# Value products of two pairs of heads as one block in an attention and top-1 expert kernel

## The chip, the core and the metric

The kernel runs on one core of a Trainium2 chip, as one launch. The metric is the device time of that core in microseconds, from first instruction to last. Engines are named as in the profile: PE (TensorE, matmuls; PEld are its weight loads), DVE (VectorE), ACT (ScalarE), POOL (GpSimd), SP (SyncE, which issues most DMA transfers here).

## The reference

```python
scores = scale * np.matmul(q, k.transpose(0, 1, 3, 2))      # 8 batches, 8 heads, 576 x 64
cum = np.cumsum(np.maximum(s, 0.0), axis=-1)
bias = -(cum[:, :, :, None] - cum[:, :, None, :])
scores = np.where(causal, -1e9, scores + np.minimum(bias, 0.0))
scores = scores - np.max(scores, axis=-1, keepdims=True)
attn = np.exp(scores)
attn = attn / (np.sum(attn, axis=-1, keepdims=True) + 1e-09)
x = np.matmul(attn, v)              # -> 4608 tokens x 512
...
e_idx = np.argmax(x @ w_gate + modality_bias[modality_id], axis=1)   # 8 experts
# for each token: its one expert, 512 -> 1024 (relu) -> 512, times the softmax weight of that expert
```

## The kernel before

Two batches of the same head make a pair: 32 pairs of heads, numbered 0 to 31, eight (the heads) to a group of two batches. Group after group is scored, and when a group is done its tokens are given to experts and scattered to lists in DRAM (`lists<-x,di` on POOL, line 841). The expert stage follows the attention.

Each pair takes nine steps (`run`). A step scores one tile of 128 queries, in the order `ORDER = (3, 7, 2, 6, 8, 1, 5, 0, 4)`: tiles 0 to 3 belong to the one batch of the pair, 4 to 7 to the other, tile 8 holds the last 64 queries of both. A score is a product in two parts, high (L376: `KA`, `QH`) and low (L398: `KB`, `QL`); tile 8 has eight of 288 columns (L416, L417). It goes to one of four PSUM banks named `sp`, in turn. DVE takes the score from there, masks it and finds the row's minimum (L400); ACT makes the exponentials and their sums (L431). `LAG = 3` steps later PE transposes the tile (L451, into one of two banks `pt`, or L466), and ACT or DVE copies it to `PT` (L455), of which there are two, for even and odd pairs.

When all nine tiles of a pair are in `PT`, `whole` issues the pair's value products (L547), two matmuls of 64 columns of V on each half of the array: 512 columns of sums in the bank `o`, the last 64 of queries in an `sp` bank called `ox`. `TD = 1` puts them one step after the last transpose, in the fifth of the nine steps of the next pair. Then ACT copies the sums to `oT` (L554), DVE the last 64 columns (L557), and PE projects `oT` by `pw` and `pq` (L350, into `xo`), which also brings them back to token order; `XLAG = 6` steps lie between the two parts of the projection.

The operands of pair p+1 are prepared while pair p is scored (`prep`): POOL rounds `KA` and `QH` (L326, two halves each) and subtracts for `QL` and the lower `KA` (L330, two halves each). There are two of each tile, so POOL must wait until pair p−1 has been scored; the raw q and k are loaded one pair earlier still. SP issues the loads, the copy of the upper half of `KA` to `KB`, and the rows of the bias (`place`: `KB<-ek`, `QL<-ek`, for pairs under 8 from SBUF, `KB<-ekd`, `QL<-eqd` later). The order on every engine is that in which the program issues, but for places where `issue_after` fixes it.

The last pair, 31, has its products in two parts (`tail`).

Of the kernel before, what the change touches and what calls it, by code (L numbers as in the profile page):

```python
# [7 lines left out]
F32 = mybir.dt.float32  # L8
# [4 lines left out]
ALU = mybir.AluOpType  # L13
# [4 lines left out]
P = 128  # L18
KW = 576
XW = 72  # L20
# [4 lines left out]
ORDER = (3, 7, 2, 6, 8, 1, 5, 0, 4)  # L25
LAG = 3
XLAG = 6
TD = 1
SPB = 4
# [13 lines left out]
class Attn:  # L43
# [3 lines left out]
    def __init__(self, ctx, tc, qkv, s, ident, wg):  # L47
        nc = tc.nc
        self.nc, self.tc, self.qkv, self.ident = nc, tc, qkv, ident
        c = self.const = ctx.enter_context(tc.tile_pool(name="aconst", bufs=1))  # L50
# [10 lines left out]
        self.KB = [c.tile([P, 2, KW], F32R, name=f"KB{u}") for u in range(2)]  # L61
        self.PT = [c.tile([P, 2, PTW], F32, name=f"PT{u}") for u in range(2)]
        self.oT = c.tile([P, 640], F32, name="oT")
        self.pw = c.tile([P, 8, 2 * XW], F32, name="pw")
        self.pq = c.tile([P, 8, XW], F32, name="pq")
        self.mk = c.tile([P, 800], F32, name="mk")
# [2 lines left out]
        self.pe, self.wall, self.last = [], None, None  # L69
        self.raw, self.V = {}, {}  # L70
        self.hold, self.act, self.sp = [None], None, None
# [12 lines left out]
        nc.sync.dma_start(self.wg, wg.rearrange("p (h e) -> p h e", e=8))  # L84
        self.V[0] = self.load_v(0)

# [16 lines left out]
        nb, last = t1.tile([P, 5], F32, name="nb"), 0.0  # L103
        end = t1.tile([P, 2], F32, name="end")
        hold = ExitStack()
        for g, w in enumerate((256, 256, 64)):
            nc.vector.tensor_tensor_scan(cum[g][:, :w], s8[:, 256 * g:256 * g + w], zz.broadcast_to([P, w]), last, ALU.add, ALU.add)
            n = (w + P - 1) // P
            nc.vector.tensor_scalar(nb[:, 2 * g:2 * g + n], cum[g][:, 0:w:P], -1.0, None, ALU.mult)
            if g < 2:  # L110
                last = end[:, g:g + 1]
# [8 lines left out]
        for c in (3, 2, 1, 4, 0):  # L120
            n = min(P * (c + 1), KW)
# [25 lines left out]
        with self.tc.issue_after(self.sp):  # L147
            self.V[1] = self.load_v(1)
        self.more = {6: self.units}
# [144 lines left out]

    def consts(self):
        nc = self.nc
        nc.gpsimd.memset(self.oT[:, 512:], 0.0)
        for t in self.PT:
            nc.vector.memset(t[64:, :, PTW - 64:], 0.0)

# [8 lines left out]
        return raw  # L309

    def load_v(self, pi):
        V = self.ld.tile([P, 2, 5, 64], F32, name="V")
        self.nc.sync.dma_start(V, self.qkv[pi, :, 4 * KW:].rearrange("p (a j d) -> p a j d", a=2, j=5))
        return V

# [48 lines left out]
    def start(self, pi, x):  # L364
        st = dict(pi=pi, h=pi % 8, x=x, s={}, high={}, PT=self.PT[pi % 2], V=self.V.pop(pi, None))
        st["mx"] = self.sm.tile([P, 10], F32, name="mx")
        st["sums"] = self.sm.tile([P, 9], F32, name="sums")
        return st
# [156 lines left out]
        if g:  # L525
            nc.vector.tensor_scalar(x[2][:, 0, :, h], xo[:, 4 * XW:5 * XW].rearrange("p (d r) -> p d r", r=2), rs[:, 8:9], None, ALU.mult)

    def whole(self, st):

        nc = self.nc  # L530
        V, PT, x, h = st["V"], st["PT"], st["x"], st["h"]
        for _ in range(TD):
            yield
        o, ox = st["o"], self.ps1.tile([P, 512], F32, name="sp", bufs=SPB)
        oT = self.oT

        pe, self.pe = self.pe, []
        for j in range(5):
            for q0, q1, t, b in ((P * j, 512, o, 0), (512, KW, ox, 512)):
                if q0 == q1:  # L540
                    continue
                for ab in range(2):
                    r = slice(64 * ab, 64 * ab + 64)
                    with ExitStack() as after:
                        for i in pe:
                            after.enter_context(self.tc.issue_after(i))
                        m = nc.tensor.matmul(t[r, q0 - b:q1 - b], V[:, ab, j, :], PT[:, ab, PTS * j + q0 if j < 4 else PTW - 64:PTS * j + q1 if j < 4 else PTW], start=j == 0, stop=j == (4 if b else 3))  # L547
                pe = [m.ins]
        self.wall = m.ins
        rs = self.sm.tile([P, 9], F32, name="rs")  # L550
        with self.tc.issue_after(self.hold[0]), self.tc.issue_after(self.act):
            nc.scalar.activation(rs, st["sums"], AF.Identity, bias=self.eps[:, :1])
            nc.vector.reciprocal(rs, rs)
        nc.scalar.copy(oT[:, :512], o)  # L554
        for ab in range(2):
            r = slice(64 * ab, 64 * ab + 64)
            nc.vector.tensor_copy(oT[r, 512 + 64 * ab:576 + 64 * ab], ox[r, :64])  # L557
        yield
        xo = self.xo
        for g in (1, 0):  # L560
            for u in range(2):
                c = 2 * g + u
                with self.tc.issue_after(self.pe[-1]):
                    self.pw_(xo[:, 2 * XW * u:2 * XW * u + 2 * XW], oT[:, P * c:P * c + P], self.pw[:, h, :], start=True, stop=True)
            if g:
                self.pw_(xo[:, 4 * XW:5 * XW], oT[:, 512:], self.pq[:, h, :], start=True, stop=True)
            src = xo[:, :4 * XW].rearrange("p (t d) -> p t d", t=4)
            rv = rs[:, 4 * g:4 * g + 4].unsqueeze(2).broadcast_to([P, 4, XW])
            nc.vector.tensor_tensor(x[g][:, :, :, h], src.rearrange("p t (d r) -> p t d r", r=2), rv.rearrange("p t (d r) -> p t d r", r=2), ALU.mult)
            if g:  # L570
                nc.vector.tensor_scalar(x[2][:, 0, :, h], xo[:, 4 * XW:5 * XW].rearrange("p (d r) -> p d r", r=2), rs[:, 8:9], None, ALU.mult)
                for _ in range(XLAG if st["pi"] % 8 < 7 and st["pi"] < 30 else 1):
                    yield

    def strict(self, k):

# [2 lines left out]
    def run(self, npair, newx, done, setup):  # L579

        bg = self.bg = []
        seq = [(pi, i) for pi in range(npair) for i in ORDER]
        sts = {}
        prev, prepg, n = [], None, len(seq)
        for k in range(n + LAG + 9):
            if k < n:
                pi, i = seq[k]
                if k % 9 == 0:
                    sts[pi] = self.start(pi, newx(pi // 8) if pi % 8 == 0 else sts[pi - 1]["x"])
                    prepg = self.prep(pi + 1) if pi + 1 < npair else None  # L590
                with self.behind() if pi or not self.pe else self.tc.issue_after(self.pe[-1]), self.strict(k):
                    exps = self.score(sts[pi], i)
                if k in setup:
                    with self.newest():
                        more = setup[k]()
                        if more is not None:
                            bg.append([more, False])
                if k == 9 * npair - 12:
                    self.V[npair - 1] = self.load_v(npair - 1)
                if k % 9 == 2 and 1 < pi < npair - 1:  # L600
                    sts[pi]["V"] = self.load_v(pi)
                if k % 9 == 4 and 0 < pi < npair - 2:
                    self.raw[pi + 2] = self.load_qk(pi + 2)
                if prepg is not None:
                    next(prepg, 0)
            for b in bg if k % 9 == QUIET and k < n else ():
                for _ in range(QSTEPS):
                    if b[1] is True:
                        with self.newest():
                            b[1] = next(b[0], None)  # L610
            for p in list(prev) if k > n else prev[:1]:
                if next(p[0], 0) == 0:
                    prev.remove(p)
                    if p[2] == 0 and p[1]["pi"] % 8 == 7:
                        bg.append([done(p[1]["pi"] // 8, p[1]["x"]), True])
            for j in () if k == LAG else (0, 1) if k == LAG + 1 else (k - LAG,) if LAG < k < n + LAG else ():
                p0, i0 = seq[j]
                if k in INNER:
                    self.inner = lambda: self.trans(sts[p0], i0)
                    continue  # L620
                with self.behind(), self.strict(k):
                    c = self.turned = self.trans(sts[p0], i0)
                if k < n and exps is not None:
                    exps(c.ins)
                if p0 < npair - 1:
                    if i0 == ORDER[-1]:
                        prev.append((self.whole(sts[p0]), sts[p0], 0))
                elif i0 in (8, ORDER[-1]):
                    g = int(i0 == 8)
                    prev.append((self.tail(sts[p0], g), sts[p0], g))  # L630
            if not prev and k >= n + LAG:
                break
            for b in list(bg):
                if b[1] is False or b[1] is True and k >= n or b[1] is not True and k >= b[1]:
                    with self.newest():
                        b[1] = next(b[0], None)
                if b[1] is None:
                    bg.remove(b)
        assert not prev
        return bg  # L640
# [983 lines left out]
```

## Time and profile before

| | |
|---|---|
| runs, us | 769.62, 769.93, 771.53 (median 769.93) |
| the profiled execution, us | 770.4 |
| its span, us | 768.7 |
| granted PE clock | 0.994 |
| busy share PE / DVE / ACT / POOL | 99% / 72% / 66% / 48% |

The attention ends near 350 us; the rest is the expert stage. A row of the timeline has the start in us, the duration in us, the engine, the line and operation, what is written and read, the shape and how many instructions the row joins; in brackets stands the engine's idle time ahead of the row and what ended it. A row of the chain has a start, a duration, the engine and the line. Instructions of PE overlap, so the distance from start to start is what one takes on the path.

### The profile page before, as it was taken

To read this page: it belongs to the slowest core of one execution; us is meant where nothing else is said; L and a number is where in the kernel's file an instruction comes from. 1 tells how busy PE (TensorE), PEld (TensorE's weight loads), DVE (VectorE), ACT (ScalarE), POOL (GpSimd) and SP (SyncE) were. 2 spreads that over 40 slices of the span, in tenths; PEclk is the share of its full clock that TensorE was granted. 3 is DMA by queue.
4 is the path that set the end of the run, shared out by engine and by line. 5 is a ranking of instruction groups with operands and counts; after the bars stand their busy time and mean duration, and the time that the engine had idled before them with its cause. 6 is when DMAs were issued, how large, how long until landed. Compare 5 with 4: busy or idle time off the path is not lost.

```text
span 768.7 us, 17191 instructions
## 1 busy us (share of the span) xinstructions
PE 758.7 (99%) x5820; PEld 663.9 (86%) x5820; DVE 556.6 (72%) x1423; ACT 504.5 (66%) x1141; POOL 367.9 (48%) x386
## 2 busy tenths in 40 slices
PE   7999999999999999999999999999999999999997
PEld 6788888888888888888899999888999998889994
DVE  7676678666776678767868787977778877887720
ACT  6988888888888888886645555655556555555410
POOL 8968987898879978996521111101011111100111
PEclk8999999999999999999999999999999999999999
DMA  7477666676567765767999987977879878786672
GB/s 232 139 232 231 203 195 195 209 246 214 177 203 216 215 200 173 241 206 203 297 310 335 319 263 234 300 242 251 290 255 273 263 242 265 243 266 221 245 268 109
DMA packets 88552, 181.05 MB, mean 236 GB/s; under 512 B 14040, under 2 KB 33626, under 8 KB 88334
## 3 DMA queue, kind: packets, MB, share of 16 engines
q1 hardware_dynamic: 82654, 159.87, 66.4%
q0 software_dynamic: 5808, 20.06, 6.7%
q8 instruction: 47, 0.77, 0.4%
q14 instruction: 43, 0.35, 0.1%
HBM read 143.43 MB, written 26.67 MB: 221 GB/s over the span
## 4 chain that ended last, share of the span: by engine, by line
PE 56%; issue 23%; DMA 16%; DVE 2%; POOL 1%; ACT 1%; POOLq 1%; SPq 0%; DVEq 0%
DMA out<-ys,oi 15%; PE pt L451 10%; PE o L547 9%; PE hp L1277 6%; PE y L1249 6%; PE sp L398 5%; PE sp L376 5%; PE ox L350 5%; PE sp L416 2%; PE sp L547 2%; PE sp L417 2%; PE pt L466 2%; DMA QL<-ek 0%; DMA wrbw<-in_w 0%; PE o L466 0%
## 5 line engine op out<-in xcount | busy, mean ns | idle before, releaser
L1262 POOL DMA_INDIRECT out<-ys,oi x36 | 41.9, 1164 | 331.1 <-ACT ys L1261 245.6
L431 ACT ACTIVATE pe<-pe,mx 128x512 f32<-128x512 f32 (+3 forms) x256 | 142.8, 560 | 21.2 <-DVE mx L400 17.2
L400 DVE CUSTOM_DVE_ANT_0 pe<-sp,mk 128x512 f32<-128x512 f32 (+3 forms) x256 | 119.1, 485 | 19.0 <-PE sp L398 14.5
L1279 ACT ACTIVATE hT<-hp 128x512 fp32r<-128x512 f32 x72 | 43.1, 599 | 96.4 <-PE hp L1277 88.1
L455 ACT COPY PT<-pt 128x512 f32<-128x512 f32 (+1 forms) x192 | 96.9, 505 | 13.7 <-PE pt L451 10.9
L451 PE MATMUL pt<-ident,pe 128*128 128x128 f32 x640 | 104.3, 277 | 0.3 <-ACT PT L455 0.2
L376 PE MATMUL sp<-KA,QH 128*128 128x256 f32 (+2 forms) x256 | 98.2, 389 | 2.0 <-POOL KA L240 2.0
L1280 DVE SCALAR_TENSOR_TENSOR hT<-hp,hT 128x512 fp32r<-128x512 f32 x72 | 49.6, 689 | 60.9 <-ACT hT L1279 60.7
L330 POOL TENSOR_TENSOR QL<-rawq,QH 64x576 fp32r<-64x576 f32 x62 | 86.9, 1420 | 0.3
L330 POOL TENSOR_TENSOR KA<-rawk,KA 64x576 fp32r<-64x576 f32 x62 | 86.5, 1414 | 0.1
L1277 PE MATMUL hp<-xT,wcb 128*128 128x256 f32 x648 | 85.7, 276 | 0.0
L398 PE MATMUL sp<-KB,QL 76*128 76x256 f32 (+2 forms) x256 | 84.2, 332 | 0.7 <-DMA QL<-ek 0.7
L547 PE MATMUL o<-PT,V 128*64 128x512 f32 (+1 forms) x496 | 84.5, 440 | 0.0
L451 PEld LDWEIGHTS pt<-ident,pe 128*128 128x128 f32 x640 | 75.8, 144 | 9.9 <-ACT PT L455 0.5
L1277 PEld LDWEIGHTS hp<-xT,wcb 128*128 128x128 f32 x648 | 79.6, 188 | 0.6
L1249 PE MATMUL y<-wcb,hT 128*128 128x512 f32 x336 | 78.9, 392 | 0.0
L1249 PEld LDWEIGHTS y<-wcb,hT 128*128 128x128 f32 x336 | 62.7, 188 | 13.4
L1277 PE MATMUL hp<-xT,wca 128*128 128x256 f32 x528 | 71.9, 276 | 0.0
L547 PEld LDWEIGHTS sp<-PT,V 128*64 128x64 f32 x620 | 38.2, 137 | 33.3 <-issue 28.8
L1277 PEld LDWEIGHTS hp<-xT,wca 128*128 128x128 f32 x528 | 65.8, 188 | 0.4
L1277 PE MATMUL hp<-xT,wcc 128*128 128x256 f32 x456 | 62.6, 277 | 0.0
L1249 PE MATMUL y<-wcc,hT 128*128 128x512 f32 x264 | 62.1, 391 | 0.0
(301 smaller groups left out, 1625.0 us busy)
## 6 DMA issues: line engine op xcount, KB each, us to landing
wrbw<-in_w SPq DMA_DIRECT2D x94, 512.0 KB
wraw<-in_w SPq DMA_DIRECT2D x50, 512.0 KB
rawq<-in_qkv SPq DMA_DIRECT2D x31, 576.0 KB
rawk<-in_qkv SPq DMA_DIRECT2D x31, 576.0 KB
V<-in_qkv SPq DMA_DIRECT2D x32, 320.0 KB
KB<-KA SPq DMA_DIRECT2D x62, 144.0 KB
xr<-lists SPq DMA_DIRECT2D x68, 128.0 KB
wcb<-in_w SPq DMA_DIRECT2D x10, 512.0 KB
```

The lines of the kernel that those rows point to most:

```text
L330: self.last = nc.gpsimd.tensor_tensor(o, i, h, ALU.subtract).ins
L376: self.pe.append(self.nc.tensor.matmul(sp[:, :nn], QH[:, q0:q0 + P], self.KA[u][:, ab, :nn], start=True, stop=False).ins)
L398: self.pe.append(nc.tensor.matmul(sp[:, :nn], QL[:EXT, q0:q0 + P], KB[:EXT, ab, :nn], start=False, stop=True).ins)
L400: ins = nc.vector.tensor_tensor_reduce(out=t[:, :n], in0=sp[:, :n], in1=self.mk[:, 512 - n:512], scale=-0.125, scalar=3.0e38, op0=ALU.add, ...
L431: self.act = nc.scalar.activation(t[:, :n], t[:, :n], AF.Exp, bias=m, scale=-1.0, accum_out=st["sums"][:, o:o + 1]).ins
L451: self.pe.append(nc.tensor.transpose(out=pt[:, o:o + P], in_=pe[:, P * j:P * j + P], identity=self.ident).ins)
L455: return cp(w[:, :, :, v:v + P], pt[:, :n * (1 + both)].rearrange("p (a j q) -> p a j q", a=1 + both, q=P))
L547: m = nc.tensor.matmul(t[r, q0 - b:q1 - b], V[:, ab, j, :], PT[:, ab, PTS * j + q0 if j < 4 else PTW - 64:PTS * j + q1 if j < 4 else PTW], ...
L1249: self.last[0] = nc.tensor.matmul(y[u], hT[:, a, f, P * u:P * u + P], W[4 + f // 2][:, c, 512 * (f % 2):512 * (f % 2) + 512], start=f == 0 ...
L1277: self.last[0] = nc.tensor.matmul(hp[:, u], W[k][:, a, f:f + P], xT[:, c, k], start=k == 0 and i == 0, stop=k == 3 and i == 2)
L1279: hi = nc.scalar.activation(hs, hp, AF.Relu)
L1280: lo = self.lo = nc.vector.scalar_tensor_tensor(hT[:, 1, 2 * m:2 * m + 2], hp, 0.0, hs.bitcast(F32), ALU.max, ALU.subtract)
```

## The change

The value products of an even pair A and the following odd pair B are issued together, in the fourth step of the next even pair; so there are 15 joined blocks (pairs 0 and 1 up to 28 and 29), pair 30 by itself and pair 31 as before. In a joined block A's 512 columns go to a further `sp` bank, B's to `o`, and the last 64 columns of both to one `ox`. There is a second `oT` tile (`oTb`), a third V buffer, and the projections of A and then B are spread over later steps by a list of lags. The scratch for descriptors of POOL's DMA transfers is 8192 bytes (16384 if nothing is given).

```diff
+        self.oTb = c.tile([P, 640], F32, name="oTb")
...
-        nc.gpsimd.memset(self.oT[:, 512:], 0.0)
+        for t in (self.oT, self.oTb):
+            nc.gpsimd.memset(t[:, 512:], 0.0)
...
-        V = self.ld.tile([P, 2, 5, 64], F32, name="V")
+        V = self.ld.tile([P, 2, 5, 64], F32, name="V", bufs=3)
...
+    def whole(self, sts):
+        nc = self.nc
+        for _ in range(TD if len(sts) == 1 else 0):
+            yield
+        ox = self.ps1.tile([P, 512], F32, name="sp", bufs=SPB)
+        oTs, rss = (self.oT, self.oTb), []
+        for n, st in enumerate(sts):
+            o = st["o"] if n == len(sts) - 1 else self.ps1.tile([P, 512], F32, name="sp", bufs=SPB)
+            self.values(st, o, ox, 64 * n)
+            rss.append(self.inverse(st))
+            nc.scalar.copy(oTs[n][:, :512], o)
+        self.wall = self.pe[-1]
+        self.pe = []
+        for n, st in enumerate(sts):
+            for ab in range(2):
+                r = slice(64 * ab, 64 * ab + 64)
+                nc.vector.tensor_copy(oTs[n][r, 512 + 64 * ab:576 + 64 * ab], ox[r, 64 * n:64 * n + 64])
         yield
...
+        last = sts[-1]["pi"]
+        lag = [1] * 4 if last % 8 == 7 or last >= 28 else [XLAG] if len(sts) == 1 else [6, 3, 6, 0]
+        if len(sts) == 2:
+            yield
+        for st, rs, oT in zip(sts, rss, oTs):
...
-                for _ in range(XLAG if st["pi"] % 8 < 7 and st["pi"] < 30 else 1):
-                    yield
+                if g or st is not sts[-1]:
+                    for _ in range(lag.pop(0)):
+                        yield
...
-                    if i0 == ORDER[-1]:
-                        prev.append((self.whole(sts[p0]), sts[p0], 0))
+                    if i0 == ORDER[-1] and (p0 % 2 or p0 == npair - 2):
+                        prev.append((self.whole([sts[p0 - 1], sts[p0]] if p0 % 2 else [sts[p0]]), sts[p0], 0))
...
-    nc = _bacc.Bacc("TRN2", target_bir_lowering=False, num_devices=1)
+    nc = _bacc.Bacc("TRN2", target_bir_lowering=False, num_devices=1, dynamic_dma_scratch_size=8192)
```

`values` holds the loops of L547 and `inverse` the lines of `rs`, both unchanged but for the columns of `ox`.

On PE, before, the block of pair 13 in pair 14 (`KA_105`, `QH_101` are the even tiles, `PT_110` the odd pair's):

```order
L416 MATMUL sp<-KA_105,QH_101 128x288
L417 MATMUL sp<-KB_107,QL_103 128x288
L547 MATMUL o<-PT_110,V 64x512 x2
L547 MATMUL sp<-PT_110,V 64x64 x2
L547 MATMUL o<-PT_110,V 64x384 x2
L547 MATMUL sp<-PT_110,V 64x64 x2
L547 MATMUL o<-PT_110,V 64x256 x2
L547 MATMUL sp<-PT_110,V 64x64 x2
L547 MATMUL o<-PT_110,V 64x128 x2
L547 MATMUL sp<-PT_110,V 64x64 x4
L451 MATMUL pt<-ident,pe_2587 128x128 x4
```

And now the middle and the end of the joined block of pairs 12 and 13 at the same place:

```order
L544 MATMUL sp<-PT_109,V 64x128 x2
L544 MATMUL sp<-PT_109,V 64x64 x4
L544 MATMUL o<-PT_110,V 64x512 x2
L544 MATMUL sp<-PT_110,V 64x64 x2
L544 MATMUL o<-PT_110,V 64x384 x2
L544 MATMUL sp<-PT_110,V 64x64 x2
L544 MATMUL o<-PT_110,V 64x256 x2
L544 MATMUL sp<-PT_110,V 64x64 x2
L544 MATMUL o<-PT_110,V 64x128 x2
L544 MATMUL sp<-PT_110,V 64x64 x4
L453 MATMUL pt<-ident,pe_2538 128x128 x4
L418 MATMUL sp<-KA_105,QH_101 128x288
```

Pair 12's products stood among pair 13's scores; now they stand among pair 14's, right ahead of pair 13's, and the eight products of tile 8 now come after the block.

On POOL, before, from the end of pair 28's preparation (odd tiles are `KA_106`, even ones `KA_105`) to pair 30's:

```order
L330 TENSOR_TENSOR KA_105<-rawk,KA_105 64x576 x2
L841 DMA lists<-x,di 38912x576 x2
L326 TENSOR_SCALAR KA_106<-rawk 128x576 x2
L326 TENSOR_SCALAR QH_102<-rawq 128x576 x2
L841 DMA lists<-x,di 38912x576
L330 TENSOR_TENSOR QL_104<-rawq,QH_102 64x576 x2
L330 TENSOR_TENSOR KA_106<-rawk,KA_106 64x576
L841 DMA lists<-x,di 38912x576
L330 TENSOR_TENSOR KA_106<-rawk,KA_106 64x576
L841 DMA lists<-x,di 38912x576
L326 TENSOR_SCALAR KA_105<-rawk 128x576 x2
```

The same stretch now:

```order
L332 TENSOR_TENSOR KA_105<-rawk,KA_105 64x576 x2
L328 TENSOR_SCALAR KA_106<-rawk 128x576 x2
L328 TENSOR_SCALAR QH_102<-rawq 128x576 x2
L865 DMA lists<-x,di 38912x576 x3
L332 TENSOR_TENSOR QL_104<-rawq,QH_102 64x576 x2
L332 TENSOR_TENSOR KA_106<-rawk,KA_106 64x576
L865 DMA lists<-x,di 38912x576
L332 TENSOR_TENSOR KA_106<-rawk,KA_106 64x576
L865 DMA lists<-x,di 38912x576
L328 TENSOR_SCALAR KA_105<-rawk 128x576 x2
```

Two scatters of the last finished group have moved from ahead of pair 29's preparation into it; pair 30's own, after the last row, has the same rows as before.

More of the change, by code (lines that the diff above doesn't have):

```diff
@@ L526, in tail, with values @@
             nc.vector.tensor_scalar(x[2][:, 0, :, h], xo[:, 4 * XW:5 * XW].rearrange("p (d r) -> p d r", r=2), rs[:, 8:9], None, ALU.mult)
-    def whole(self, st):
+    def values(self, st, o, ox, b0):
         nc = self.nc
-        V, PT, x, h = st["V"], st["PT"], st["x"], st["h"]
-        for _ in range(TD):
-            yield
-        o, ox = st["o"], self.ps1.tile([P, 512], F32, name="sp", bufs=SPB)
-        oT = self.oT
+        V, PT = st["V"], st["PT"]
         pe, self.pe = self.pe, []
         for j in range(5):
-            for q0, q1, t, b in ((P * j, 512, o, 0), (512, KW, ox, 512)):
+            for q0, q1, t, b in ((P * j, 512, o, 0), (512, KW, ox, 512 - b0)):
                 if q0 == q1:
@@ L548, in whole, with inverse @@
                 pe = [m.ins]
-        self.wall = m.ins
+        self.pe = pe
+    def inverse(self, st):
+        nc = self.nc
         rs = self.sm.tile([P, 9], F32, name="rs")
@@ L553, in whole @@
             nc.vector.reciprocal(rs, rs)
[L554 to L557, printed above, removed]
+        return rs
+    def whole(self, sts):
+        nc = self.nc
+        for _ in range(TD if len(sts) == 1 else 0):
[13 more added lines that the diff above has]
+                nc.vector.tensor_copy(oTs[n][r, 512 + 64 * ab:576 + 64 * ab], ox[r, 64 * n:64 * n + 64])
@@ L558, in whole @@
         yield
         xo = self.xo
[L560 to L571, printed above, removed]
-                for _ in range(XLAG if st["pi"] % 8 < 7 and st["pi"] < 30 else 1):
-                    yield
+        last = sts[-1]["pi"]
@@ new lines, in whole @@
+        lag = [1] * 4 if last % 8 == 7 or last >= 28 else [XLAG] if len(sts) == 1 else [6, 3, 6, 0]
+        if len(sts) == 2:
+            yield
+        for st, rs, oT in zip(sts, rss, oTs):
+            x, h = st["x"], st["h"]
+            for g in (1, 0):
+                for u in range(2):
+                    c = 2 * g + u
+                    with self.tc.issue_after(self.pe[-1]):
+                        self.pw_(xo[:, 2 * XW * u:2 * XW * u + 2 * XW], oT[:, P * c:P * c + P], self.pw[:, h, :], start=True, stop=True)
+                if g:
+                    self.pw_(xo[:, 4 * XW:5 * XW], oT[:, 512:], self.pq[:, h, :], start=True, stop=True)
+                src = xo[:, :4 * XW].rearrange("p (t d) -> p t d", t=4)
+                rv = rs[:, 4 * g:4 * g + 4].unsqueeze(2).broadcast_to([P, 4, XW])
+                nc.vector.tensor_tensor(x[g][:, :, :, h], src.rearrange("p t (d r) -> p t d r", r=2), rv.rearrange("p t (d r) -> p t d r", r=2), ALU.mult)
+                if g:
+                    nc.vector.tensor_scalar(x[2][:, 0, :, h], xo[:, 4 * XW:5 * XW].rearrange("p (d r) -> p d r", r=2), rs[:, 8:9], None, ALU.mult)
+                if g or st is not sts[-1]:
+                    for _ in range(lag.pop(0)):
+                        yield
```

## The prediction

> **What bounds the kernel now.** I read the page's busy shares first, then the stretch of the regular pairs in the table of windows, the chain that ended last, and the timeline of PE, POOL and ACT around one pair.
>
> ```profile
> span 768.7 us, 17191 instructions
> PE 758.7 (99%) x5820; PEld 663.9 (86%) x5820; DVE 556.6 (72%) x1423; ACT 504.5 (66%) x1141; POOL 367.9 (48%) x386
> 37.18:347.51 310.33, 310.29 (x2764) 263.12 (x2762) 222.62 (x897) 258.55 (x773) 267.41 (x270) 1.00 0.68 209
> 500.00:600.00 100.00, 100.00 (x648) 90.52 (x647) 77.73 (x94) 55.68 (x71) 8.93 (x8) 1.00 0.82 265
> 26.84 1.01 PE o L547 x4
> ...
> 154.97 1.01 PE o L547 x4
> ...
> 165.62 1.01 PE o L547 x4
> ...
> 347.80 1.01 PE o L547 x4
> ```
>
> The windows' columns are the stretch, its length, then busy time and count of PE, PEld, DVE, ACT and POOL. From 37 to 348 us PE has 0.04 us without a matmul; POOL is busy 267.4 of 310.3 us and ACT 258.6. The 100 us of the MoE stage also hold a full PE, and that stage's work is the same after the change, so what the attention stage gains or loses moves the end by the same amount. The value products occur 31 times in the chain, the first at 26.84 and the last at 347.80: 320.96 / 30 = 10.70 us per pair, 10.65 between the two middle rows. PE binds on average; where the change leaves less PE work between two waits, POOL and ACT are near.
>
> **The seam: what is saved.** One pair's value products on PE, with what stands ahead and behind:
>
> ```profile
> 154.54 0.30 PE L416 MATMUL sp<-KA,QH 128*128 128x288 f32 x1
> 154.68 0.29 PE L417 MATMUL sp<-KB,QL 76*128 76x288 f32 x1
> 154.90 1.08 PE L547 MATMUL o<-PT,V 128*64 128x512 f32 x4
> 155.81 0.28 PE L547 MATMUL sp<-PT,V 128*64 128x64 f32 x4
> 155.93 0.82 PE L547 MATMUL o<-PT,V 128*64 128x384 f32 x4
> ...
> 157.46 0.40 PE L547 MATMUL sp<-PT,V 128*64 128x64 f32 x8
> 157.79 0.66 PE L451 MATMUL pt<-ident,pe 128*128 128x128 f32 x4
> 158.20 0.36 PE L376 MATMUL sp<-KA,QH 128*128 128x256 f32 x1
> ...
> 161.60 0.60 PE L451 MATMUL pt<-ident,pe 128*128 128x128 f32 x4
> 161.96 0.48 PE L376 MATMUL sp<-KA,QH 128*128 128x512 f32 x1
> ```
>
> The second column is an instruction's own time, which overlaps the next; cost is the distance of starts. Entry: 154.68 to 154.90 is 0.22 us where a 288-wide product inside the run takes 0.14, so 0.08; the 512-wide group takes 0.91 to the next start where 4/3 of the 384-wide group's 0.64 would be 0.85, so 0.06. Exit: the 64-wide eight take 0.33 where twice the four's 0.12 would be 0.24, so 0.09; the first transposes take 0.41 where those at 161.60 take 0.36, so 0.05. Together 0.28 to 0.29 us that a block of this column shape costs beyond its products. 31 entries become 16: 15 × 0.29 = **−4.4 us**. Bounds: −3.5 (15 × 0.23) if the step inside a joined block, from pair A's 64-wide products to pair B's 512-wide ones, keeps the 0.06 as at the entry; −4.4 if it costs nothing. I take −4.4, since the step from 155.81 to 155.93, also from 64 to wide within the block, shows none. The Trainium skill ("TensorEngine Tiling (Array Packing)", Key Properties) says that changing the tiling mode drains TensorE. By that rule alone only the two changes of mode are saved, 0.23 us without the 0.06 of the first wide group, and the sum would be 0.9 higher; the trace has the 0.29, and no run here shows yet which part stays.
>
> **What the joining takes away: time in the odd pairs.** Without its block a pair's stretch on PE is 10.65 − 2.97 = 7.68 us (2.97 is 2.89 of the block's stretch, 154.90 to 157.79, the 0.08 of entry; the rest of the seam lies inside). Blocks go to even pairs, so odd pairs shrink to 7.68 and even ones grow to 13.3. POOL works one pair ahead: while an odd pair is scored it makes the next even pair's KA, QH, QL. Its chain starts about 0.5 us after the last score that reads those tiles, and its last KA half must be there for the second 512-wide L376 of the next pair.
>
> ```profile
> 150.01 1.32 POOL L326 TENSOR_SCALAR KA<-rawk 128x576 fp32r<-128x576 f32 x2
> 152.76 1.05 POOL L841 DMA_INDIRECT lists<-x,di  x1 [0.17 <-issue]
> 153.84 2.81 POOL L330 TENSOR_TENSOR QL<-rawq,QH 64x576 fp32r<-64x576 f32 x2
> 156.61 2.77 POOL L330 TENSOR_TENSOR KA<-rawk,KA 64x576 fp32r<-64x576 f32 x2
> ...
> 263.48 2.79 POOL L330 TENSOR_TENSOR KA<-rawk,KA 64x576 fp32r<-64x576 f32 x2
> 268.84 0.48 PE L376 MATMUL sp<-KA,QH 128*128 128x512 f32 x1
> POOL KA L326 <- PE sp L376: 26.2, 15, 3.0
> ```
>
> - Pair 14: the chain runs 150.01 to 159.38, and PE needs it at 161.96 (quoted above): 2.58 to spare. Pair 24: 266.27 against 268.84, 2.57. Minus 2.97, both are 0.39 short. Four even chains carry one scatter (14, 16, 22, 24), so 4 × 0.39 = 1.6; if POOL starts 0.1 sooner, free of the queue that held it until 150.01, it is 1.2. I take **+1.2**. A chain without a scatter is 1.2 shorter and keeps 0.4 or more. The 15 waits of the last row are slack POOL has now; they shrink.
> - Pair 30 has two scatters in its chain:
>
> ```profile
> 322.63 1.32 POOL L326 TENSOR_SCALAR KA<-rawk 128x576 fp32r<-128x576 f32 x2
> 330.78 0.99 POOL L841 DMA_INDIRECT lists<-x,di  x1 [0.17 <-issue]
> 331.80 1.43 POOL L330 TENSOR_TENSOR KA<-rawk,KA 64x576 fp32r<-64x576 f32 x1
> 333.51 0.48 PE L376 MATMUL sp<-KA,QH 128*128 128x512 f32 x1
> ```
>
> It ends at 333.23, 0.28 before the need; minus 2.97 that is 2.7 short. Pair 29 now carries three scatters together, but in a 13.3 us stretch, and pair 30's start, 0.6 later than it could be at 322.63, may come that much sooner: 2.1. I take **+2.4**.
> - Pair 2, 4 and 6, whose chains start late:
>
> ```profile
> 27.99 2.78 POOL L330 TENSOR_TENSOR KA<-rawk,KA 64x576 fp32r<-64x576 f32 x2
> 33.83 0.48 PE L376 MATMUL sp<-KA,QH 128*128 128x512 f32 x1
> 45.12 1.31 POOL L326 TENSOR_SCALAR KA<-rawk 128x576 fp32r<-128x576 f32 x2 [3.07 <-DMA ekd<-ek]
> 50.42 2.79 POOL L330 TENSOR_TENSOR KA<-rawk,KA 64x576 fp32r<-64x576 f32 x2
> 55.08 0.48 PE L376 MATMUL sp<-KA,QH 128*128 128x512 f32 x1
> 67.02 1.31 POOL L326 TENSOR_SCALAR KA<-rawk 128x576 fp32r<-128x576 f32 x2 [1.87 <-DMA rawk<-in_qkv]
> ```
>
> Pair 2: 33.83 − 30.77 = 3.06 to spare; minus 2.97 and a further memset of about 0.2 ahead on POOL, 0.1 to 0.5 short, I take **+0.3**. Pair 4: 55.08 − 53.21 = 1.87, so 1.1 short; pair 6, chain 67.02 + 8.09 = 75.11 against a need at 76.36 (the 55.08 plus two pairs), 1.7 short, if these starts, which wait for loads, stay where they are against PE. The loads stand in SP's queue behind saves and placements that wait for PE. If the loads land at fixed times the two cost up to 2.0 together beyond pair 2's (what is lost once isn't lost again); if they move with PE's releases and land in time, 0. Half: **+1.2** for the two, the middle of 0 and 2.0 with the longer stretch after them.
>
> **ACT and the other costs.**
>
> ```profile
> 154.62 0.61 ACT L431 ACTIVATE pe<-pe,mx 128x384 f32<-128x384 f32 x1
> 155.13 0.19 ACT L431 ACTIVATION_READ_ACCUMULATOR pe<-pe,mx 128x1 f32 x1
> 157.67 0.59 ACT L554 COPY oT<-o 128x512 f32<-128x512 f32 x1 [0.92 <-PE o L547]
> 154.90:157.79 2.89, 2.89 (x38) 1.75 (x37) 0.78 (x5) 1.97 (x7) 2.89 (x3) 1.00 0.77 258
> 157.79:165.56 7.77, 7.77 (x64) 7.32 (x60) 6.34 (x25) 6.87 (x21) 7.40 (x9) 1.00 0.85 274
> ```
>
> Outside the block ACT works 6.87 us of 7.77 (last row), in it 1.97 of 2.89, and it carries exponentials into the block (154.62) that it clears while PE multiplies. 8.84 us a pair, less the copy of the sums (0.59) and some 0.3 for the sums' small row, leave 7.95 of exponentials and PT copies; rows that stand back to back overlap by about 0.1 in the trace (154.62 + 0.61 ends 0.1 after the next row's start), which makes it nearer 7.7: in an odd pair ACT is level with PE's 7.68. Over two pairs it has 17.7 at most of 21 us, since the joined block is 5.6 us with little to do. A walk through one double pair, with each row's distance as its cost, gives PE a wait of 0.1 us for a transpose bank (0 to 0.25). Where POOL stalls PE, ACT catches up, so eight of 15 count: **+0.8** (0 to 3.8, if all of them and the upper end).
>
> - Extra sums: pair A's 512 columns hold one more of the four sp banks, and the 64-wide ones of both share one. The banks' next users come after the eight 288-wide products or later; ACT copies pair A's during pair B's 2.7 us. 0, bounds −0.1 and +0.2 per block; the second ends below ACT's walk, which has it in.
> - DVE copies four 64-column pieces after the block where it copied two: 0.46 us more, once per two pairs, beside PE. The projections are the same count, spread over later steps: their weights are 64-column moves already in the pair's 7.68 and cost as before, 0.
> - Pair A's products wait longer and V lives longer; the third V buffer lets its load go out without that wait: 0. It passes KB's placement in SP's order by some transfers of 320 KB: within the 0.4 that an unburdened chain keeps.
> - The group work that DVE does once per eight pairs falls in odd pairs now: 0.1 to 0.2 each at three places, hidden behind sp banks; 0, at most +0.6.
> - 8 KB scratch for POOL's scatters instead of 16: every scatter row above takes 0.98 to 1.06 us and shows no wait but 0.17 of issue; 0. The trace shows no other size, so bounds 0 and one scatter's 1.06 for each of 32 if it stalled; nearest to the rows, 0.
>
> Sum: −4.4 + 1.2 + 2.4 + 0.3 + 1.2 + 0.8 = **+1.5 us**. The profiled execution took 770.4 (its span of 768.7 and 1.7 around it), 0.5 over the median of 769.93; 771.9 against it is **771.4** against the median, +0.2%. The bound of no change is 0.3%, 2.3 us: 767.6 to 772.2.
>
> **Rivals.**
> - *The saving stands alone.* POOL's chains and the loads move up by as much as PE's need, or the waits run while PE has another delay: 769.9 − 4.4 = 765.5, 767 with pair 30's wait at 1.5 left. For it: POOL waits for PE 26.2 us in 15 places, so most chains have room. Against: pair 30's chain is 10.6 us of pure instructions. 0.28.
> - *POOL binds the odd pairs.* The sum with its upper ends: pairs 14 to 24 1.6, pair 30 2.7, pair 2 0.5, pairs 4 and 6 2.0 is 6.8 − 4.4 + 0.8 = +3.2, 773.1; with another 0.4 on each of the five chains with exactly 0.4 left, 775. It decides from 2.3 us over the saving, that is chains 6.7 us late in all. For it: 8.15 us of chain against 7.68 of stretch. 0.22.
> - *ACT binds the odd pairs.* If copies out of the product banks and exponentials, not PE, set the odd stretch: 15 × 0.25 = 3.8 beside POOL's 5.1 gives +4.5, 774.4; with copies 0.4 late, 776. For it: 7.7 of 7.68 us; against: ACT itself waits 0.92 us for PE in each block. 0.10. The Trainium skill (same page, Performance Considerations, PSUM Bottleneck) says that tiling speeds TensorE but not the copying out of PSUM, which may become the bottleneck; the 0.92 us says that it isn't one now, and no trace of before shows a pair without a block, where the rule would bite.
> - *The joined block keeps its seam*, because PE waits at pair B for its last PT copy: pair A's 2.7 us lie between, so only the price changes; with 0.29 kept, the time is 769.9 + 5.9 = 775.8. It is within the two slower cases' chance.
>
> **How the numbers follow.** No change 0.40 (the sum), the saving alone 0.28, POOL 0.22, ACT 0.10. The time is the sum's, 771.4. Its own range is 767.6 to 772.9. For 8 in 10 the range reaches from 766.0, inside the saving's case, to 775.5, short of the worst ends of POOL and ACT.
>
> **What would show it.** In the trace after: 16 entries of L544, about 5.6 us each, with the seam only at their ends; first 512-wide L378 of even pairs behind POOL's last KA: 0.3 late at pairs 14, 16, 22, 24 and over 2 at pair 30; idle PE of about 6 us in all below 348 us, absent now; ACT idle inside the joined block. If PE shows no idle, the POOL step is wrong and the saving stands; if odd pairs each lose 0.3 us or more to ACT or sp banks, the walk is wrong; and if the seam stays at 31 × 0.29, its cause was another.

## The result

The changed kernel is slower: 782.74 us (median of 4 runs, 781.09 to 783.63) against 769.84, a ratio of 1.0149 with a 95% interval of 1.0118 to 1.0181. The forecast was 771.4 with a range from 766.0 to 775.5. The profiled execution of the changed kernel took 781.09 us, 10.7 more than that of before (770.4); the trace below explains those 10.7. The medians differ by 12.9; the other 2.2 us are the choice of executions: the profiled one of before ran 0.6 above its median of 769.84, that of the changed kernel 1.65 below its own. In the rounds of the experiments 11 of 51 executions of the kernel before took 776 to 779 us at the same granted clock, and as the ratios are taken with them, they come out lower than the medians alone would give.

The page of the changed kernel, and its chain of work, where a joined block is one row of pair A (`sp`) and two of pair B:

```profile
span 779.0 us, 17156 instructions
PE 762.9 (98%) x5820; PEld 660.3 (85%) x5820; DVE 553.2 (71%) x1423; ACT 498.7 (64%) x1141; POOL 368.1 (47%) x387
33.11 2.88 PE sp L544 x36
...
55.91 2.89 PE sp L544 x36
...
164.98 2.88 PE sp L544 x36
167.86 0.86 PE o L544 x4
...
186.41 2.88 PE sp L544 x36
...
208.86 2.88 PE sp L544 x36
...
230.87 2.88 PE sp L544 x36
...
318.16 2.88 PE sp L544 x36
...
342.19 2.88 PE sp L544 x36
...
358.65 1.01 PE o L544 x4
```

The distance from block to block is a double pair. Two pairs of before took 21.27 us where nothing else happens, 21.4 to 21.7 where a group of eight ends:

```profile
144.35 1.01 PE o L547 x4
...
165.62 1.01 PE o L547 x4
```

Now the plain double pairs take 21.4 (164.98 to 186.41 is 21.43), those that hold pairs 9, 17 and 25, behind a group's end, 22.45 (186.41 to 208.86), the next ones, with pairs 11, 19 and 27, 22.01, the first 22.80, and the one with pair 30 24.03 (318.16 to 342.19). Pair 30's block starts at 358.65 instead of 347.80: all 10.85 us of the loss arise in the attention.

What waits is told by the list of waits (engine, what waits, for what: us in all, times, the longest) and the timeline:

```profile
PEld sp L378 <- POOL KA L332: 6.7, 8, 1.7
PE sp L378 <- POOL KA L332: 4.7, 6, 1.4
PEld pt L453 <- ACT PT L457: 4.4, 18, 0.6
PEld pt L468 <- ACT PT L457: 2.0, 6, 0.7
ACT oTb L568 <- PE o L544: 31.3, 15, 2.2
```

```profile
335.89 0.50 PE L378 MATMUL sp<-KA,QH 128*128 128x512 f32 x1 [0.31 <-POOL KA L332]
338.49 0.50 PE L378 MATMUL sp<-KA,QH 128*128 128x512 f32 x1 [1.42 <-POOL KA L332]
...
327.82 1.32 POOL L328 TENSOR_SCALAR KA<-rawk 128x576 fp32r<-128x576 f32 x2
337.02 1.41 POOL L332 TENSOR_TENSOR KA<-rawk,KA 64x576 fp32r<-64x576 f32 x1
```

In the kernel before no score waited for these KA rows, and PE's loads and transposes at `pt` waited under 1 us for ACT's copies in all. At pair 30 POOL's chain ends at 338.43, and PE's second 512-wide score starts at 338.49, right behind it. ACT waits 31.3 us for PE inside the 15 joined blocks, 2.1 each: time that it has there and, as the window rows at the end show, not in the odd pairs.

### The profile page after: what moved, and what is told of

Same layout as the page of the kernel before. It is cut to its first block, busy times and chain, and to the rows that moved or that the text cites. A ratio compares the mean times of both kernels' runs of the same rounds, so it can differ in the third digit from the quotient of the medians.

```text
span 779.0 us, 17156 instructions
## 1 busy us (share of the span) xinstructions
PE 762.9 (98%) x5820; PEld 660.3 (85%) x5820; DVE 553.2 (71%) x1423; ACT 498.7 (64%) x1141; POOL 368.1 (47%) x387
## 4 chain that ended last, share of the span: by engine, by line
PE 49%; issue 24%; DMA 17%; POOL 5%; ACT 2%; DVE 1%; POOLq 1%; SPq 0%; ACTq 0%; DVEq 0%
DMA out<-ys,oi 17%; PE pt L453 8%; PE sp L544 7%; PE hp L1301 7%; PE y L1273 6%; PE o L544 4%; PE ox L352 4%; PE sp L378 4%; PE sp L400 4%; PE sp L418 2%; PE sp L419 2%; POOL KA L332 2%; PE pt L468 2%; POOL QL L332 1%; ACT pe L433 1%
## 5 line engine op out<-in xcount | busy, mean ns | idle before, releaser
L433 ACT ACTIVATE pe<-pe,mx 128x384 f32<-128x384 f32 (+3 forms) x256 | 143.0, 562 | 13.2 <-DVE mx L402 12.7
L402 DVE CUSTOM_DVE_ANT_0 pe<-sp,mk 128x384 f32<-128x384 f32 (+3 forms) x256 | 119.8, 484 | 18.2 <-PE sp L400 12.6
L544 PEld LDWEIGHTS sp<-PT,V 128*64 128x64 f32 x860 | 45.8, 137 | 36.7 <-issue 26.9
L544 PE MATMUL sp<-PT,V 128*64 128x64 f32 (+1 forms) x860 | 64.4, 282 | 0.0
```

The source lines that it names most:

```text
L402: ins = nc.vector.tensor_tensor_reduce(out=t[:, :n], in0=sp[:, :n], in1=self.mk[:, 512 - n:512], scale=-0.125, scalar=3.0e38, op0=ALU.add, ...
L433: self.act = nc.scalar.activation(t[:, :n], t[:, :n], AF.Exp, bias=m, scale=-1.0, accum_out=st["sums"][:, o:o + 1]).ins
```

## The experiments

All numbers of blocks below are distances of chain rows as above; times are medians, and ratios are taken against the kernel before on the same chip, one of several.

**The memory alone.** Kernel before with

```diff
+        self.oTb = c.tile([P, 640], F32, name="oTb")
+        for t in (self.oT, self.oTb): nc.gpsimd.memset(t[:, 512:], 0.0)
+        V = self.ld.tile([P, 2, 5, 64], F32, name="V", bufs=3)
+    nc = _bacc.Bacc(..., dynamic_dma_scratch_size=8192)
```

> The kernel before with the change's memory alone: second oT tile, third V buffer, 8 KB of descriptor scratch; the value products stay one pair at a time. If these three cost nothing, 769.9 within 0.3% (767.6 to 772.2), 31 value blocks at 10.65 us. If the scratch or V's earlier loads cost the loss, 778 or more, with longer scatter rows on POOL or later raw loads.

Measured 770.39 us, ratio 0.9979 (0.9941 to 1.0017), value blocks still 10.64 apart. Second oT tile, third V buffer and small scratch cost nothing by themselves that shows here; the loss is in the joining.

**A shorter chain for even pairs.**

```diff
-            low(QL[lo, a, :KW], rq[lo, a], QHf[lo, a, :KW])
+            if pi % 2 or pi < 2:
+                low(QL[lo, a, :KW], rq[lo, a], QHf[lo, a, :KW])
```

> The changed kernel, but the two subtractions for QL are left out for even pairs from 2 on (their QL keeps pair 0's values), so POOL's chain for even pairs is 2.8 us shorter and nothing else changes. If POOL's late chains are most of the 15 us lost, the waits at pairs 2, 4, 6, 10, 14, 16, 18, 22, 24, 26 and 30 go: the loss falls by 7 to 10 us, 773 to 776, double pairs 14 and 16 at 21.0 to 21.1 instead of 21.40, pair 30's double pair at 21.6 instead of 24.0. If ACT, DVE and the finer mix of PE's rows are most, it falls by under 3 us, 780 or more.

Measured 773.91 us, ratio 1.0017 (0.9982 to 1.0052): 8.8 us less than the changed kernel's 782.74, which was taken in another round. Its chain:

```profile
32.26 2.88 PE sp L545 x36
...
53.78 2.89 PE sp L545 x36
...
161.62 2.89 PE sp L545 x36
...
182.82 2.88 PE sp L545 x36
...
204.40 2.88 PE sp L545 x36
...
226.41 2.88 PE sp L545 x36
...
312.40 2.88 PE sp L545 x36
...
334.17 2.88 PE sp L545 x36
...
350.62 1.01 PE o L545 x4
```

Pair 30's block is 8.03 us earlier than in the changed kernel. By double pair: pair 30's 24.03 to 21.77, so 2.26; pairs 10, 18 and 26 0.70, 0.87 and 0.88; pairs 14, 16, 22 and 24 0.19 to 0.24 each; the first block comes 0.85 sooner, and the first three double pairs lose 1.6 less together. POOL's late chains are 8.0 us of the loss. What is left in the attention with the short chain is 2.8 us over before (350.62 against 347.80), although a seam is saved in each double pair.

**Control: the same work off POOL, for odd pairs.** The condition is `pi % 2 == 0 or pi < 2`.

> Control: QL's subtractions left out for odd pairs instead of even ones, the same work less on POOL, but in the long stretches. If the loss is the length of the even pairs' chains against the short odd stretches, at most 2 us are gained (the chain ahead ends sooner): 781 to 783. If POOL's work as such disturbs the other engines, the gain is like that of the even pairs, 773 to 776.

Measured 781.44 us, ratio 1.0113 (1.0038 to 1.0187), double pairs as in the changed kernel (21.40, 22.45, 22.02), but for pair 30's, 23.56 instead of 24.03, whose chain can start sooner. It isn't POOL's work, nor what it disturbs, but its length in the short stretch.

**Spread lags at a group's end.**

```diff
-        lag = [1] * 4 if last % 8 == 7 or last >= 28 else ...
+        lag = [1] * 4 if last >= 28 else ...
```

> The changed kernel with the spread lags (6, 3, 6, 0) also for the pairs that end a group (7, 15, 23), where it packs the projections into the steps right after the block. If the packed projections delay the scores that free KA and so POOL's chain for pairs 10, 18 and 26, these double pairs fall from 22.45 to 21.4 to 21.7 and the time by 2 to 3 us, 780. If the group's DVE work is the cause, it only moves: no change within 1 us.

Measured 805.73 us, ratio 1.0389 (1.0316 to 1.0462). The total isn't what was asked: the third group's lists come later, the double pair with pair 30 grows from 24.03 to 31.14 and the expert stage starts late. POOL stands 7.9 us there until DVE has the list positions (`di`), PE 4.2 us for KA, and the granted clock is 0.65 from 340 to 350 us, so that the block there takes 4.92 us in the chain instead of 2.88. The double pair asked about does answer:

```profile
99.20 2.89 PE sp L544 x36
...
120.41 2.88 PE sp L544 x36
...
143.51 2.88 PE sp L544 x36
...
166.20 2.88 PE sp L544 x36
```

It falls from 22.45 to 21.21; the two behind it, which now hold the group's work, rise from 22.00 and 21.40 to 23.10 and 22.69. Three together go from 65.85 to 67.00. The other two behind a group's end fall to 21.21 as well. So the packed projections do delay POOL's chain for pairs 10, 18 and 26, and what they avoid costs more.

**The groups' choice of experts in long pairs only.**

```diff
-            for b in bg if k % 9 == QUIET and k < n else ():
-                for _ in range(QSTEPS):
+            for b in bg if k % 18 == QUIET and k < n else ():
+                for _ in range(2 * QSTEPS):
```

> The changed kernel with the groups' DVE work (the choice of experts) put only into even pairs, the long ones that hold the joined block, ten of its steps at a time instead of five. If that work in short pairs makes the six slow double pairs (22.45 and 22.0), they fall to 21.4 to 21.7 each and the time by 3 to 5 us, 778 to 780. If the loss there is POOL's alone, the 22.45 stay and at most 1.5 us are gained.

Measured 804.81 us, ratio 1.0354 (1.0265 to 1.0442), again by the late third group (27.08 for the double pair with pair 30). The double pairs at 22.0 and 22.45 didn't fall (22.73 and 22.16, then 23.32 where the scatters moved to). That DVE's work falls in a short pair is not what makes them slow, or moving it costs as much; which of the two is open.

**Tile 8's transposes ahead of the last score.** In the changed kernel PE's rows have four of tile 8's transposes behind the pair's last score, in the kernel before ahead of it.

```diff
+        if k >= 72 and k % 9 == 8:
+            after = ExitStack()
+            for i in self.pe[-2:]:
+                after.enter_context(self.tc.issue_after(i))
+            return after
```

> The changed kernel, from pair 8 on with the transposes of tile 8 held ahead of the pair's last score, as they stand in the kernel before (the change has them behind it, so that the next pair's first 512-wide score follows a transpose). If this order costs the 0.25 to 0.3 us per double pair that remain with POOL's chain shortened, the double pairs that don't wait for POOL fall by 0.25, those that do wait keep their length, and the time falls by 1 to 3 us. If ACT is late for these transposes, PE waits for them in the new place instead: no gain or a loss.

> The same order, and QL's subtractions left out for even pairs as in the run with the short chain. If the order costs 0.25 to 0.3 per double pair, regular double pairs fall from 21.19 to 20.9 to 21.0 and the time to about 771. If ACT is late, 773.9 or more.

Measured 788.65 us (ratio 1.0201, 1.0126 to 1.0276) and 786.23 us (1.0169, 1.0095 to 1.0244): 6 and 12 us more than the same kernels without the line, which ran in other rounds. Plain double pairs are 21.86 to 21.92 in both, so POOL is not what they wait for. The second kernel on PE and ACT at the end of even pair 14, 4 us behind its block:

```profile
174.64 0.28 PE L401 MATMUL sp<-KB,QL 76*128 76x256 f32 x1
174.76 0.27 PE L469 MATMUL o<-ident,pep 128*64 128x128 f32 x1
175.17 0.66 PE L469 MATMUL pt<-ident,pep 128*128 128x128 f32 x4
...
174.16 0.50 ACT L434 ACTIVATE pe<-pe,mx 128x256 f32<-128x256 f32 x1
174.66 0.46 ACT L458 COPY PT<-pt 128x384 f32<-128x384 f32 x1
175.01 0.52 ACT L434 ACTIVATE pe<-pe,mx 128x256 f32<-128x256 f32 x1
```

The four transposes start 0.41 us after the single one, in the kernel before one step of these is 0.11: they need a `pt` bank, and ACT copies it out from 174.66 on, at the end of 1.7 us of work without a gap. At the end of odd pair 15 the same step is 0.48 (182.83 to 183.32). So PE waits for ACT in both kinds of pairs. The line doesn't give quite the order of before: there the four come first and the single one behind them.

**That order in the kernel before.** Tile 8's four transposes are put behind the last score for pairs 8 to 30, the single one stays:

```diff
+                if cut and k == j + LAG:
+                    late = j
+                    with self.behind(), self.strict(k):
+                        self.trans(sts[p0], i0, ((4, 1),))
+                    continue
...
+                    c = self.turned = self.trans(sts[p0], i0, ((0, 4),) if cut else ((0, 4), (4, 1)))
```

> The kernel before, with one thing of the changed kernel's order put in: for pairs 8 to 30 tile 8's four full transposes stand behind the pair's last score (the single one stays ahead of it), as PE's rows show in the changed kernel. Value products, POOL's chains and the rest are as before. The rows of the two kernels' regular double pairs differ by 0.25 us in these steps alone (a score after a transpose instead of after a score, one more change of kind). If the order by itself costs that, each pair grows by 0.12 us, 23 pairs by 2.8 us: 772 to 773.5. If the 0.25 us is a wait for ACT that only the changed kernel has, 769.5 to 771.

Measured 769.41 us, ratio 0.9966 (0.9937 to 0.9995), a plain double pair 21.28 as before:

```profile
145.00 1.01 PE o L547 x4
...
166.28 1.01 PE o L547 x4
```

One double pair, where the edit sets in (68.86 to 91.53), has 1.4 us more, with PE waiting for loads of q and k. The order alone costs nothing; my reading of the rows, that a score after a transpose is dearer, is refuted as the cause. In the kernel with the short chain the same steps are 0.23 us longer per double pair, by the starts of PE's rows: the steps from a low score to tile 8's transposes 0.62 us where this run has 0.49, and within those transposes 0.77 where it has 0.66. It is the four transposes that start late each time, not the single one.

**ACT's work cut, in odd and in even pairs.** With the short chain and

```diff
+            m = 16 if st["pi"] > 1 and st["pi"] % 2 == 1 and c > 1 else P
+            return cp(w[:, :, :, v:v + m], ...[:, :, :, :m])
```

or `% 2 == 0`.

> The kernel with the short chain (QL's subtractions left out for even pairs), and in odd pairs ACT's four large copies to PT (tiles 2, 3, 6, 7) take only 16 of each 128 queries, the rest of PT keeping older values: about 1 us less of ACT in each short stretch. If ACT, level with PE there, makes what is left of the loss (tile 8's transposes late, the finer mix of rows), regular double pairs fall from 21.19 to 20.9 to 21.0 and the time from 773.9 to 768 to 771. If the mix of rows has another cause, such as DVE or the order alone, 773 or more.

> Control: the short chain, and the same four copies cut in even pairs, whose stretches hold the joined block and leave ACT idle for about 4 us. If it is ACT's work in the short stretches that counts, 773 to 774 as with the short chain alone. If ACT's work in all counts, the same gain as in odd pairs.

Measured 773.53 us (ratio 1.0039, 1.0025 to 1.0053) and 792.19 us. The second time can't be read: the older values send tokens to other experts, and the expert stage has 44 more matmuls. In the attention pair 30's block starts at 350.39 and 349.82, against 350.62 with the short chain alone. Plain double pairs fall from 21.19 to 21.08 (161.51 to 182.59) and to 21.10, by 0.1 in both. Those at 21.6 stay in both; those at 22.0 stay with the odd pairs' cut (21.90 to 22.18) and fall to 21.7 with the even pairs'. From the first joined block to pair 30's the two take 1.0 and 1.4 us less than with the short chain alone; the first block itself comes 0.8 and 0.6 later. With the odd pairs' cut, tile 8's transposes of even pair 14 and then of odd pair 15:

```profile
171.36 0.28 PE L401 MATMUL sp<-KB,QL 76*128 76x256 f32 x1
171.54 0.66 PE L470 MATMUL pt<-ident,pep 128*128 128x128 f32 x4
...
178.72 0.29 PE L401 MATMUL sp<-KB,QL 76*128 76x256 f32 x1
178.84 0.60 PE L470 MATMUL pt<-ident,pep 128*128 128x128 f32 x4
```

Pair 14's are as late as without the cut (0.18 behind the score, and 0.66 long), pair 15's are on time (0.12, 0.60) and ahead of the last score, as before; with the even pairs' cut it is pair 14's that are on time. So the 0.23 us of a plain double pair are ACT's, about half in each kind of pair, and so are 0.3 of three long ones in the even pairs; the theory that ACT's work in the short stretches makes the whole rest is refuted.

**A seam put back.**

```diff
+            if n < len(sts) - 1:
+                for _ in range(2):
+                    with self.tc.issue_after(self.pe[-1]):
+                        self.pe.append(nc.tensor.transpose(out=ox[:, 128:256], in_=self.ident, identity=self.ident).ins)
```

> The changed kernel with two full-width transposes of the identity between pair A's and pair B's products, into columns of the bank that nothing reads: a seam put back into each of the 15 joined blocks, in the long stretches where nothing else should be late. Two such transposes take 0.2 to 0.3 us by the steps within a group. If the change of shape costs 0.29 us, each double pair grows by 0.5 to 0.6 and the time by 7 to 9 us, to 790 to 792; if the shape costs nothing, by 3 to 4.5 us, to 786 to 787.

Measured 789.13 us, ratio 1.0244 (1.0227 to 1.0261), 6.4 more than the changed kernel. Its block:

```profile
168.08 2.88 PE sp L544 x36
171.33 1.01 PE o L544 x4
```

By the starts of PE's rows pair B's products follow pair A's after 3.25 us, in the changed kernel after 2.79, and B's first 512-wide products take 0.05 more. From its first product to the row behind it the block takes 6.14 us instead of 5.62. Of the 0.52 two transposes are 0.22 by the step within a group, 0.11 each; 0.30 is the change of shape. Pair 30's block starts 7.15 later, 0.48 for each of 15. The seam is real and the joining does save it.

**Half of the even pairs' QL on DVE**, a complete kernel, with tile 8's transposes ahead:

```diff
+            if a and pi > 1 and pi % 2 == 0:
+                nc.vector.tensor_tensor(QL[lo, a, :KW], rq[lo, a], QHf[lo, a, :KW], ALU.subtract)
```

> A complete kernel: tile 8's transposes first, and for even pairs one of the two subtractions for QL on DVE instead of POOL. POOL's chain is 1.4 us shorter, more than the 0.3 to 0.8 us that pairs 10 to 26 lack; pair 30 still lacks 0.5 or so. DVE has about 0.7 us more in the short stretches, where it is busy 6 to 7 of 8 us. If POOL's chain and the order are the loss, 773 to 777. If DVE is nearly the bound there, 780 or more.

Measured 808.08 us, ratio 1.0457 (1.038 to 1.0534); two double pairs that are plain in the changed kernel have 27.6 and 27.0. Since it also has the line that cost 6 us, it doesn't tell what DVE's share is; no version with joined blocks beat the kernel before.

## Why the prediction was wrong

The 10.85 us of loss in the attention are about −4.5 (seams saved), +8.0 (POOL) and +7.3 (what is left, ACT in part). The forecast had −4.4, +5.1 and +0.8.

- **The saving** held: PE's steps into and out of the blocks are 0.33 us shorter in a plain double pair with the short chain (0.43 us, where before two blocks had 0.75). Against that stands 0.03 for the steps between score and transpose where a block stood before, so 0.30 net; 0.29 was forecast, and the seam put back costs 0.30. The −4.4 is −4.5.
- **Pair 30** was forecast at +2.4 and measured 2.26; **pairs 14, 16, 22, 24** at +1.2 and measured 0.86 in all. The mechanism, a chain of fixed length in a stretch that is 2.97 us shorter, is shown by the short chain and its control.
- **Pairs 10, 18, 26** is a step that failed: "the projections are the same count, spread over later steps", cost 0, and unburdened chains "keep 0.4 or more". At a group's end the lags are all 1, so the projections are packed into the steps right after the block, and part of one stands, with tile 8's transposes, between the two scores that free KA's halves:

```profile
196.76 0.67 POOL L328 TENSOR_SCALAR KA<-rawk 128x576 fp32r<-128x576 f32 x1 [3.30 <-PE sp L378]
198.36 0.67 POOL L328 TENSOR_SCALAR KA<-rawk 128x576 fp32r<-128x576 f32 x1 [0.92 <-PE sp L378]
...
205.90 0.50 PE L378 MATMUL sp<-KA,QH 128*128 128x512 f32 x1 [0.53 <-POOL KA L332]
```

POOL's second half waits 0.92 us more, the spare 0.4 is gone, and PE waits: 2.5 us in all. I had the list of lags in the diff and read only its last entry.
- **The early pairs** were forecast at 1.5 (0.3 for pair 2, 1.2 for pairs 4 and 6) and measured 2.5, and the step that was written, loads that stay where they are, is not what the rows show:

```profile
29.67 0.50 PE L378 MATMUL sp<-KA,QH 128*128 128x512 f32 x1 [1.34 <-POOL KA L332]
42.92 1.31 POOL L328 TENSOR_SCALAR KA<-rawk 128x576 fp32r<-128x576 f32 x2 [0.67 <-PE sp L400]
65.71 1.31 POOL L328 TENSOR_SCALAR KA<-rawk 128x576 fp32r<-128x576 f32 x2 [1.86 <-PE sp L378]
```

The chains of pairs 4 and 6 start behind PE's scores, at 42.92 instead of 45.12 and at 65.71 instead of 67.02: the loads did move up. Pair 2 alone costs 0.85 by the short chain. PE is ready for its first score at 28.33, 4.7 us sooner than before (33.01) and not 2.97; pair 1 now holds neither pair 0's block nor its projections. PE then waits 1.34 us for POOL. The other 1.6 go with the short chain too, 1.3 of them in the double pair with pair 4.
- **POOL in all**: 5.1 forecast, 8.0 measured. The rival "POOL binds the odd pairs" came true, but only beside ACT's. Its 6.8 was short by the packed projections; the further 0.4 that it allowed on each of five chains would cover the 8.0, without naming them as the cause.
- **ACT and the rest** is the term that was missed most: +0.8 forecast. The balance is 10.85 + 4.5 − 8.0, some 7.3 us. Plain double pairs have 0.23 of it each, tile 8's transposes at `pt` banks that come late (by the run that has their order in the kernel before), as ACT's rival had it with its 0.25; those at a group's end and the first ones have 0.45 to 0.7 each (one 0.26), and I had put the groups' DVE work at 0 to 0.6 in all. The walk through one plain double pair (0.1, upper end 0.25) looked at the kind of pair that lost least. That POOL's stalls would hide ACT's lateness was wrong too, since the short chain leaves the rest standing. The two cuts of ACT's copies take 1.0 and 1.4 us away; some 5 us of the 7.3 have no cause that a run shows. The window rows show the squeeze that I read from an average of 17.7 in 21 us:

```profile
171.00:178.00 7.00, 7.00 (x56) 6.63 (x55) 5.89 (x24) 5.83 (x19) 6.61 (x8) 1.00 1.01 397
178.00:185.00 7.00, 7.00 (x54) 6.38 (x54) 5.62 (x23) 7.00 (x23) 6.64 (x6) 1.00 0.81 235
```

In the lower row, most of it odd pair 15, ACT (fourth engine) is busy for all 7.00 us and POOL 6.64. A full ACT isn't the whole account, though: in the upper row, the end of even pair 14 and the first scores of pair 15, ACT is busy 5.83 us, and tile 8's transposes come as late there (0.18 us behind the score against 0.19 in pair 15, 0.12 before). The Trainium skill ("TensorEngine Tiling (Array Packing)", PSUM Bottleneck) says that tiling speeds up TensorE but not the copying out of PSUM, and that the copy may become the bottleneck after a 4x speedup. The `pt` waits here are such waits for a copy, though the change sped up no matmul, and they make a part of the loss (0.1 us of a plain double pair went with fewer copies in either kind of pair); POOL, which the rule doesn't speak of, had the larger part that is shown.
- What made the six double pairs behind a group's end longer by 0.45 to 0.7 even with the short chain, the saved seam added back, stays open: moving the groups' work didn't lower them, and cutting ACT's copies took 0.3 from three of the six. In PE's rows scores and transposes are split there into more and shorter groups.
- The account of the kernel ahead of the prediction calls the order that of the program. The rows show otherwise: one edit of lags or lines moves tile 8's transposes, projections and scatters far from it, so an edit that should move one thing moved several (805 us twice).

## What to carry to other kernels

Joining short blocks on the busiest engine saves its seams, here 0.3 us per joint, but it makes the stretches between uneven, and each helper engine whose chain has a fixed length must then fit the shortest stretch, not the mean. Before such a change, list for every helper the spare time of its chain in each stretch (2.6 us here) against what the move takes away (3.0 us), also in the odd places: group ends, the first pairs, the last ones. And read the rows of all kinds of stretches that the program builds, not only of the plain one.

## What was not expected of the hardware

A row of transposes that comes late by a few hundredths costs PE twice here: in the kernel with the short chain the steps from the score to tile 8's four transposes grew by 0.06 to 0.07 us each, and the first step within them by 0.05 more, 0.23 in a double pair; PE's own waits for ACT's copies are 1.0 us in that whole run. And the same order without lateness cost nothing (21.28 against 21.28), so what looked like a price of mixing kinds of matmuls was, in these rows, a price of waiting.
